# Fifteen products for eighteen in the gate and value stage of a SwiGLU block behind a gated linear attention

## The chip, the cores and the metric

The kernel runs on one core of a Trainium2 chip. The metric is the device time of one execution in microseconds. Three runs of the kernel before gave a median of 641.87 us (641.79 to 645.67). The profile was taken of one more execution.

## The reference

An attention with a decaying state (4 batches, 8 heads, 768 positions, 48 channels a head) is followed by a SwiGLU block (384 to 1536 to 384 channels). The inputs q, k, v and f_logit are float32; the three weights come as float64 and are turned into float32 on the chip.

```
f = 1.0 / (1.0 + np.exp(-f_logit))
for t in range(S):
    state = f[:, :, t, :, None] * state + np.einsum('bhd,bhe->bhde', k[:, :, t], v[:, :, t])
    y[:, :, t] = np.einsum('bhd,bhde->bhe', q[:, :, t], state)
x = y.transpose(0, 2, 1, 3).reshape(B * S, H * D)
g = x @ w_gate
silu = g * (1.0 / (1.0 + np.exp(-g)))
out = (silu * (x @ w_val)) @ w_out
```

## The kernel before

**Tiling.** The 768 positions are cut into six blocks of 128. Block c holds these 128 positions of all four batches, 512 tokens in all (TB), laid channels first in `xT[c]` as three slices of 128 channels (KT = 3). A unit is one batch of one block; there are 24, four to a block. This text counts blocks from 1 to 6, so block 1 is c = 0 in the code; units are counted from 0, and unit 8 is the first of block 3.

**Staging.** The attention of block 1 comes first. From then on the MLP of a block runs mixed with the attention of the block after it: `take_turns` (L885) deals out the pieces of the MLP and between them the 16 attention steps of the next block (`attention_steps`, L612). Block 6 has no attention beside it. The first two blocks transpose f, k and q on TensorE; from block 3 on (`SQUARES`, L315) they are loaded in a layout that VectorE transposes in 32 by 32 squares (L494, L514, L515). Their sigmoid (L493) is on ScalarE, which also does the Silu of the MLP and copies out of PSUM.

**The MLP of block 1** is plain (`mlp_plain`, L641): for each 128 of the 1536 hidden channels, three matmuls of 512 tokens for gate and three for val. **The MLP of blocks 2 to 6** is `mlp_seven` (L730). The hidden channels are cut into halves, the tokens into halves of 256 (TH), and of the three channel slices the first two form, with these halves, a 2 by 2 by 2 product that takes seven multiplications in place of eight; the third slice is added by four plain ones. `pair(j)` makes one pair of hidden tiles (128 channels of either half, so six pairs a block) by 11 products; each product is two matmuls of 256 tokens, one for gate and one for val, into the two halves of one PSUM bank (`add`, L752). VectorE adds the parts up in SBUF (`plus`, L702). The weight sums it needs are made once, after block 1, on VectorE (`weight_sums`, L711), the token sums once a block (`token_sums`, L737). A hidden tile `h[j]` has four parts of 256 tokens.

**The output product** (`down_seven`, L798) also takes seven products for eight, over sums `s1`, `s2` of hidden parts that `hidden_sums` makes behind each pair. Its four pieces `one` to `four` end a block.

**What sets the order.** [...] The order in the code is a wish: the framework that builds the program may move an instruction that is ready ahead of one that is not, by durations that it assumes. `in_order` (L621) pins the order of TensorE's instructions within a pair or an output piece. In the trace such moves can be seen: in block 6 four matmul instructions of `two` (`o<-ws,ht`, 611.65 us) run between the two halves of `one`.

**Memory.** [...] The pools of the raw inputs, the gates, tails and four v tiles live as long as the kernel; only the staging of the weights (`wst`) is given up after block 1, and the weight sums take its place. The squares layout lies over the raw inputs (`rooms`, L334). `load_after` (L606) starts the loads of a coming unit: two units ahead in the first two blocks, one ahead from block 3 on, and the loads of unit 8 during unit 7.

Of the kernel before, what the change touches and what calls it, by code (L numbers as in the profile page):

```python
# [289 lines left out]
def short_path(ctx, tc, ident, least, judge, q, k, v, f_logit, moe_w_gate, moe_w_val, moe_w_out, out):  # L290
# [29 lines left out]
    ffn = ctx.enter_context(tc.tile_pool(name="ffn", bufs=2))  # L320
    early = ctx.enter_context(ExitStack())
    wst = early.enter_context(tc.tile_pool(name="wst", bufs=2))
    aps = ctx.enter_context(tc.tile_pool(name="aps", bufs=4, space=bass.MemoryType.PSUM))
    fps = ctx.enter_context(tc.tile_pool(name="fps", bufs=4, space=bass.MemoryType.PSUM))
# [9 lines left out]
    rooms = {nm: const.tile([128, NRAW * H * W], FP32, tag=f"{nm}raw", name=f"{nm}raw") for nm in "qkf"}  # L334
    raw = {nm: [rooms[nm][:, i * H * W:(i + 1) * H * W].rearrange("t (h d) -> t h d", d=W) for i in range(NRAW)]
# [7 lines left out]
    gates = [const.tile([128, HP * N1 + 2], FP32, tag=f"gates{i}", name=f"gates{i}") for i in range(NROT)]  # L343
    tails = [const.tile([128, HP * N1 + 2], FP32, tag=f"tails{i}", name=f"tails{i}") for i in range(NROT)]
# [25 lines left out]
    vs = [const.tile([128, H, W], FP32, tag=f"v{i}", name=f"v{i}") for i in range(NV)]  # L370
# [3 lines left out]
    w_gate = const.tile([128, KT, DFF], FP32, tag="w_gate", name="w_gate")  # L374
    w_val = const.tile([128, KT, DFF], FP32, tag="w_val", name="w_val")
# [11 lines left out]
    RUN = NI * D  # L387

# [7 lines left out]
    def load(u):  # L396
# [11 lines left out]
        nc.sync.dma_start(out=vs[u % NV][:, :, 0:D], in_=v[b, :, rows, :].rearrange("h t d -> t h d"))  # L408
# [66 lines left out]

    def bank(name):
        return aps.tile([128, 512], FP32, tag="a", name=name)

    def attention(u):
        b, c = units[u]  # L480
        fr, kr, qr = (raw[nm][u % NRAW] for nm in "fkq")
        v_ = vs[u % NV]
        gate, tail = (x[u % NROT] for x in (gates, tails))
# [122 lines left out]
    def load_after(u):  # L606

        for w, ahead in ((u + 1, True), (u + 2, False)):
            if w < len(units) and (units[w][1] >= SQUARES) == ahead:
                load(w)  # L610
# [10 lines left out]
    def in_order(since, engines):  # L621

        start = len(traced)
        while traced[start - 1] is not since:
            start -= 1
        for engine in engines:
            mine = [ins for ins in traced[start:] if ins.engine == engine]
            for a, b in zip(mine, mine[1:]):
                tc.add_manual_dep(b, a.name, mybir.DependencyInfo(mybir.DependencyClass.NoSync,
                                                                  mybir.DependencyReason.DATA), reason="order")  # L630
# [67 lines left out]

    sums = {}
    down_sums = {}  # L700

    def plus(dst, a, b):  # L702
        nc.vector.tensor_tensor(dst, a, b, ALU.add)  # L703

    def minus(dst, a, b):
        nc.vector.tensor_tensor(dst, a, b, ALU.subtract)

    def temps(shape):
        return (comb.tile(shape, FP32, tag="u", name="u", bufs=2), comb.tile(shape, FP32, tag="u5", name="u5"))

    def weight_sums():  # L711
        for nm, w in (("g", w_gate), ("v", w_val)):
            s = comb.tile([128, 3, FH], FP32, tag=f"s{nm}", name=f"s{nm}")
            a11, a12, a21, a22 = w[:, 0, 0:FH], w[:, 1, 0:FH], w[:, 0, FH:DFF], w[:, 1, FH:DFF]
            plus(s[:, 0, :], a21, a22)
            minus(s[:, 1, :], s[:, 0, :], a11)
            minus(s[:, 2, :], a12, s[:, 1, :])
            minus(a21, a11, a21)
            sums[nm] = s
# [78 lines left out]
    def down_seven(c, h):  # L798
# [36 lines left out]
        def one():  # L835
# [9 lines left out]
            for j in range(NP):  # L845
                hidden_sum_4(j)
# [194 lines left out]
```

## Time and profile before

| what | us |
|---|---|
| median of 3 runs | 641.87 |
| the profiled execution | 642.91 |
| its span, first to last instruction | 641.2 |
| TensorE busy | 632.4 |
| VectorE busy | 471.0 |
| ScalarE busy | 186.6 |
| GpSimd busy | 22.4 |

The stages of the profiled execution, cut where TensorE's work changes (TensorE is busy for the whole of each stage but the first, the last, and 0.2 us of block 5):

| stage | from, to | us | VectorE busy | ScalarE busy |
|---|---|---|---|---|
| attention of block 1 | 0.0, 35.9 | 35.9 | 27.0 | 13.2 |
| block 1 | 35.9, 149.3 | 113.4 | 99.7 | 51.2 |
| block 2 | 149.3, 251.0 | 101.7 | 80.9 | 33.9 |
| block 3 | 251.0, 352.5 | 101.5 | 77.2 | 29.4 |
| block 4 | 352.5, 454.0 | 101.5 | 77.2 | 29.4 |
| block 5 | 454.0, 551.8 | 97.8 | 64.6 | 18.2 |
| block 6, gate and val | 551.8, 607.9 | 56.1 | 35.4 | 9.5 |
| block 6, output | 607.9, 641.2 | 33.3 | 8.9 | 1.8 |

In the profile PE is TensorE, PEld its weight loads, DVE VectorE, ACT ScalarE, POOL GpSimd, SP the engine whose queue issues most loads. A line number is that of kernel.py, and a helper's line stands for all its callers: L760 is the matmul in `add` of a pair, L824 that of the output product, L703 `plus`, L706 `minus`, L768 ScalarE's copy of the first product, L775 and L790 the Silus. A float32 matmul stands as two instructions, so a product of a pair (gate and val) counts four. [...]

### The profile page before, as it was taken

The page shows a single profiled execution, that of the slowest core. Times are in us where ns is not written, and L with a number is a line of the kernel's source. Part 1 is how long each engine was busy: PE and PEld are TensorE (multiplying, and loading weights), DVE is VectorE, ACT ScalarE, POOL GpSimd, SP SyncE. Part 2 cuts the span into 40 slices and gives each one's busy share as a digit, 9 for nine tenths or more (in the row PEclk, how much of TensorE's full clock was granted, in tenths as well). Part 3 has the DMA queues.
Part 4 walks back from the last instruction along what each step waited for, and adds up shares of the span by engine and source line. Part 5 has one row for each costly group of instructions (what it writes and reads, how often), then busy time and mean ns, then how long its engine had stood idle before and what let it go on. Part 6 is the DMA issues. An engine that isn't in the chain of part 4 may idle for free.

```text
span 641.2 us, 10398 instructions
## 1 busy us (share of the span) xinstructions
PE 632.4 (99%) x4014; PEld 522.3 (81%) x4014; DVE 471.0 (73%) x802; ACT 186.6 (29%) x284; POOL 22.4 (3%) x39
## 2 busy tenths in 40 slices
PE   8999999999999999999999999999999999999996
PEld 5954555667888899888999888899888889988896
DVE  6889779988987875896966787877497862366631
ACT  1566366204632212523221614130321210021100
POOL 1000000000000010010000010000000000000000
PEclk9999999999999999999999999999999999999999
DMA  9987456333230324130324321132411001100001
GB/s 193 234 212 225 127 141 206 102 81 101 67 92 6 94 67 132 50 75 26 75 52 131 91 49 50 32 80 65 123 38 49 15 24 23 54 0 1 0 1 54
DMA packets 98393, 51.89 MB, mean 81 GB/s; under 512 B 56864, under 2 KB 92192, under 8 KB 98336
## 3 DMA queue, kind: packets, MB, share of 16 engines
q1 hardware_dynamic: 95024, 46.63, 28.7%
q10 hardware_dynamic: 3312, 4.52, 2.0%
q8 instruction: 33, 0.54, 0.4%
q14 instruction: 24, 0.20, 0.1%
HBM read 42.47 MB, written 4.72 MB: 74 GB/s over the span
## 4 chain that ended last, share of the span: by engine, by line
PE 98%; DMA 1%; DVE 0%; SPq 0%; issue 0%
PE p L760 32%; PE o L824 19%; PE c L760 13%; PE o L671 5%; PE val L647 5%; PE gate L647 5%; PE sc L535 4%; PE y L565 3%; PE o L877 3%; PE y L561 2%; PE kt L542 2%; PE dS L589 2%; PE y L582 1%; DMA fraw<-in_f_logit_dram 1%; PE idle L356 1%; PE fTp L488 1%
## 5 line engine op out<-in xcount | busy, mean ns | idle before, releaser
L703 DVE TENSOR_TENSOR rest<-u,p 128x512 f32<-128x512 f32 x90 | 61.2, 685 | 43.8 <-PE p L760 43.4
L760 PE MATMUL p<-xT,w_val 128*128 128x256 f32 x240 | 71.4, 379 | 0.0
L760 PE MATMUL p<-xT,w_gate 128*128 128x256 f32 x240 | 71.4, 379 | 0.0
L703 DVE TENSOR_TENSOR u<-u,p 128x512 f32<-128x512 f32 x90 | 61.9, 687 | 10.4 <-PE p L760 8.5
L824 PE MATMUL o<-w_out,h 128*128 128x192 f32 x360 | 62.0, 329 | 0.0
L790 ACT ACTIVATE h<-rest 128x768 f32<-128x768 f32 x30 | 25.3, 844 | 123.6 <-DVE rest L703 123.6
L824 PEld LDWEIGHTS o<-w_out,h 128*128 128x128 f32 x360 | 58.2, 190 | 1.7 <-ACT u L842 1.1
L760 PE MATMUL c<-xT,w_gate 128*128 128x256 f32 x180 | 54.9, 387 | 0.0
L760 PE MATMUL c<-xT,w_val 128*128 128x256 f32 x180 | 53.5, 379 | 0.0
L760 PEld LDWEIGHTS p<-xT,w_val 128*128 128x128 f32 x240 | 45.6, 190 | 6.2
L760 PEld LDWEIGHTS p<-xT,w_gate 128*128 128x128 f32 x240 | 45.6, 190 | 6.2
L537 DVE TENSOR_TENSOR A<-sc,causal 128x512 f32<-128x512 f32 x48 | 31.5, 685 | 10.4 <-PE sc L535 10.4
L760 PEld LDWEIGHTS c<-xT,w_val 128*128 128x128 f32 x180 | 34.2, 190 | 4.6
L527 POOL TENSOR_TENSOR decayed<-state,tails 128x192 f32<-128x192 f32 x20 | 19.7, 986 | 504.3 <-DVE state L593 360.2
L760 PEld LDWEIGHTS c<-xT,w_gate 128*128 128x128 f32 x180 | 32.5, 190 | 5.2 <-issue 0.9
L760 PE MATMUL p<-xs,sv 128*128 128x256 f32 x120 | 35.7, 379 | 0.0
L760 PE MATMUL p<-xs,sg 128*128 128x256 f32 x120 | 35.7, 379 | 0.0
L791 DVE TENSOR_TENSOR h<-h,rest 128x768 f32<-128x768 f32 x30 | 28.8, 962 | 9.1 <-ACT h L790 9.1
L768 ACT COPY u<-c 128x512 f32<-128x512 f32 x30 | 17.4, 581 | 53.8 <-PE c L760 32.1
L647 PE MATMUL val<-xT,w_val 128*128 128x512 f32 x72 | 32.3, 594 | 0.0
L647 PE MATMUL gate<-xT,w_gate 128*128 128x512 f32 x72 | 32.3, 594 | 0.0
L502 DVE TENSOR_TENSOR_SCAN tails<-gates,ones 128x516 f32<-128x516 f32 x24 | 29.4, 1224 | 3.9 <-POOL decayed L527 2.1
(127 smaller groups left out, 1076.6 us busy)
## 6 DMA issues: line engine op xcount, KB each, us to landing
fraw<-in_f_logit_dram SPq DMA_DIRECT2D x64, 96.0 KB, 3.0
kraw<-in_k_dram SPq DMA_DIRECT2D x64, 96.0 KB, 2.2
qraw<-in_q_dram SPq DMA_DIRECT2D x64, 96.0 KB, 2.2
v<-in_v_dram SPq DMA_DIRECT2D x24, 192.0 KB, 3.5
w<-in_moe_w_gate_dram SPq DMA_DIRECT2D x6, 768.0 KB, 4.6
w<-in_moe_w_val_dram SPq DMA_DIRECT2D x6, 768.0 KB, 5.1
w<-in_moe_w_out_dram SPq DMA_DIRECT2D x6, 768.0 KB, 5.6
out_dram<-ob ACTq DMA_DIRECT2D x23, 192.0 KB, 2.5
```

The costliest lines, as they stand in the source:

```text
L502: nc.vector.tensor_tensor_scan(tail[:, 0:n][:, ::-1], gate[:, 0:n][:, ::-1], ones[:, ::-1], 1.0, op0=ALU.mult, op1=ALU.add)
L527: nc.gpsimd.tensor_tensor(decayed[:, :, 0:D], states[b], whole.broadcast_to((128, HP, D)), ALU.mult)
L535: nc.tensor.matmul(sc[par][:, a * C:(a + 1) * C], lhsT=kT[r, a, :], rhs=qT[r, a, :], start=True, stop=True)
L537: nc.vector.tensor_tensor(A[:, par], sc[par].rearrange("p (a t) -> p a t", t=C), causal.unsqueeze(1).broadcast_to((128, HP, C)), ALU.mult)
L565: nc.tensor.matmul(place(a, par), lhsT=v_[:, 2 * a + par, :], rhs=A[:, par, a, :], start=False, stop=a >= HP - 2, skip_group_check=True)
L647: nc.tensor.matmul(p, lhsT=w[:, i, j * 128:(j + 1) * 128], rhs=xT[c][:, i, :], start=(i == 0), stop=(i == KT - 1))
L671: nc.tensor.matmul(p, lhsT=h[n // 2][:, n % 2 * 2 + b // 2, b % 2 * C:(b % 2 + 1) * C], rhs=w_out[:, j, :], start=(n == 0), stop=(n == NF ...
L703: nc.vector.tensor_tensor(dst, a, b, ALU.add)
L760: nc.tensor.matmul(p[:, n, :], lhsT=lhsT, rhs=rhs, start=first and n == 0, stop=last, skip_group_check=True)
L790: nc.scalar.activation(h[j][:, 1:4, :], rest[:, :, 0, :], AF.Silu)
L791: nc.vector.tensor_tensor(h[j][:, 1:4, :], h[j][:, 1:4, :], rest[:, :, 1, :], ALU.mult)
L824: nc.tensor.matmul(p[:, n, :], lhsT=lhsTs[j][:, n * C:(n + 1) * C], rhs=rhs[:, j, :], start=first and j == 0 and n == 0, stop=last and j = ...
```

## The change

In blocks 2 to 6 `mlp_fifteen` takes the place of `mlp_seven`. The hidden channels are cut into thirds of 512 (`NG`), the three channel slices all take part, and the tokens stay in halves: a 3 by 3 by 2 product with fifteen multiplications in place of eighteen. `triple(j)` makes six hidden parts (128 channels of each third, both token halves), so a block has four triples, each cut into three pieces of five products.

The products of a triple run in the order of `PRODUCTS`. Six are summed up in one PSUM bank (A, two buffers), five in another (B, one buffer), two stand alone (o), and two are summed in a bank c (o and c share two buffers). Where a result needs a sum as it stands midway, ScalarE copies the bank to SBUF, and the next product of that chain is added into the bank afterwards. VectorE combines the copies. `chained` pins the order of a triple's matmuls.

The weight sums are 16 operations over both weight matrices, in place but for six new tiles; the columns of triples 0 and 2 are made by GpSimd at the end of block 1's gate and val stage, those of triples 1 and 3 by VectorE after block 1. The triples run in the order 0, 2, 1, 3. There are eleven token sums a block for four. The output product is unchanged but for where its hidden sums are made.

Raw inputs, second gates and tails, two v tiles and the old PSUM pools are given up after block 1. The squares rooms are new tiles made then (`make_rooms`, with a memset on GpSimd), the loads of unit 8 are issued then, the attention of blocks 3 to 6 has one gates tile, one tails tile and two v tiles, and it has three PSUM banks for four; the MLP has five for four.

```diff
@@ -318,10 +318,13 @@
+    sums_pool = ctx.enter_context(tc.tile_pool(name="sums", bufs=1))
+    first_pool = early.enter_context(tc.tile_pool(name="first", bufs=1))
-    aps = ctx.enter_context(tc.tile_pool(name="aps", bufs=4, space=bass.MemoryType.PSUM))
-    fps = ctx.enter_context(tc.tile_pool(name="fps", bufs=4, space=bass.MemoryType.PSUM))
+    aps = early.enter_context(tc.tile_pool(name="aps", bufs=4, space=bass.MemoryType.PSUM))
+    fps = early.enter_context(tc.tile_pool(name="fps", bufs=4, space=bass.MemoryType.PSUM))
...
+    def make_rooms(pool):
+        for nm in "fkq":
+            rooms[nm] = pool.tile([128, Q + HP * RUN], FP32, tag=f"{nm}squares", name=f"{nm}squares")
+            nc.gpsimd.memset(rooms[nm][:, HP * RUN:], 0.0)
...
@@ -605,9 +622,9 @@
-        for w, ahead in ((u + 1, True), (u + 2, False)):
-            if w < len(units) and (units[w][1] >= SQUARES) == ahead:
-                load(w)
+        w = u + (1 if units[u][1] >= SQUARES else 2)
+        if w < len(units) and (units[w][1] >= SQUARES) == (w == u + 1):
+            load(w)
...
@@ -696,27 +715,61 @@
+    def weight_sums(odd, engine):
+        w, e = weight_parts()
+        w = {n: every_second(t, odd) for n, t in w.items()}
+        e = [every_second(t, odd) for t in e]
...
+        sub(e[0], a11, a12)
+        add(e[1], a12, a33)
+        add(e[1], e[1], a13)
+        sub(e[2], e[1], a11)
+        sub(e[3], e[0], a13)
+        add(e[4], a21, a32)
+        sub(e[5], a12, a21)
+        sub(a11, a12, a23)
+        add(a13, e[3], a21)
+        add(e[3], e[3], a23)
+        add(a13, a13, a31)
+        sub(a13, a13, a33)
+        sub(a21, a22, a21)
+        add(a22, a22, a23)
+        add(a22, a22, a32)
+        sub(a31, a32, a31)
...
+    PRODUCTS = [("A", "a11", "t14"), ("B", "a23", "t8"), ("o", "a21", "b22"),
+                ("A", "a12", "t2"), ("B", "e3", "b32"), ("o", "e0", "t1"),
+                ("A", "e5", "t9"), ("B", "e2", "t5"), ("c", "a13", "b11"),
+                ("A", "e4", "t4"), ("B", "a33", "t15"), ("c", "a31", "t10"),
+                ("A", "a32", "t11"), ("B", "e1", "t3"), ("A", "a22", "b21")]
...
+        def triple(j):
+            cols = slice(j * 128, (j + 1) * 128)
...
+            def product(r):
+                name, a, b = PRODUCTS[r]
+                fresh = name == "o" or name not in p
+                if fresh:
+                    p[name] = both(name)
+                for n in range(2):
+                    nc.tensor.matmul(p[name][:, n, :], lhsT=weights_of[a][:, n, cols], rhs=tokens[b],
+                                     start=fresh and n == 0, stop=True, skip_group_check=True)
...
+            def aside(name):
+                return copy(name, "aside", bufs=3)
+
+            def finish(i, n, src):
+                dst = out_part(i, n, j)
+                nc.scalar.activation(dst, src[:, 0, :], AF.Silu)
+                nc.vector.tensor_tensor(dst, dst, src[:, 1, :], ALU.mult)
+
+            def some(n, m):
+                for r in range(n, m):
+                    product(r)
+                    if r == 0:
+                        got[11] = copy("A", "c11", bufs=2)
+                    elif r == 1:
+                        got[22] = copy("B", "c22")
+                    elif r == 2:
+                        minus(got[22], p["o"], got[22])
+                    elif r == 3:
+                        got[12] = copy("A", "c12")
+                    elif r == 4:
+                        plus(got[12], got[12], aside("B"))
+                    elif r == 5:
+                        minus(got[12], p["o"], got[12])
+                        finish(0, 1, got[12])
+                    elif r == 6:
+                        minus(got[22], got[22], aside("A"))
+                        finish(1, 1, got[22])
+                    elif r == 7:
+                        got[32] = copy("B", "c32")
+                    elif r == 8:
+                        got[31] = copy("c", "c31")
+                    elif r == 9:
+                        plus(got[32], got[32], aside("A"))
+                    elif r == 10:
+                        minus(got[31], got[31], aside("B"))
+                    elif r == 11:
+                        minus(got[32], got[32], p["c"])
+                        finish(2, 1, got[32])
+                    elif r == 12:
+                        minus(got[31], got[31], aside("A"))
+                        finish(2, 0, got[31])
+                    elif r == 13:
+                        plus(got[11], got[11], p["B"])
+                        finish(0, 0, got[11])
+                    else:
+                        finish(1, 0, p["A"])
+
+            return [lambda n=n: chained(made, lambda: some(n, n + 5)) for n in (0, 5, 10)]
...
+        order = list(range(0, NJ, 2)) + list(range(1, NJ, 2))
+        pieces = [token_sums] + [f for j in order for f in triple(j)]
+        half = 1 + 3 * (NJ // 2)
+        ready = [sorted({(i * NJ + j) % NP for i in range(KT) for j in range(n, NJ, 2)}) for n in range(2)]
+        pieces.insert(half, lambda: [hidden_sums(n) for n in ready[0]])
+        pieces.append(lambda: [hidden_sums(n) for n in ready[1]])
...
@@ -953,15 +1063,22 @@
-            pieces = hidden + last
+            pieces = hidden + [lambda: weight_sums(0, nc.gpsimd)] + last
...
         if c == 0:
             early.close()
             comb = ctx.enter_context(tc.tile_pool(name="comb", bufs=1))
-            weight_sums()
+            banks.append(ctx.enter_context(tc.tile_pool(name="bps", bufs=3, space=bass.MemoryType.PSUM)))
+            banks_a, banks_b, banks_o = (
+                ctx.enter_context(tc.tile_pool(name=f"{n}ps", bufs=k, space=bass.MemoryType.PSUM))
+                for n, k in (("A", 2), ("B", 1), ("o", 2)))
+            make_rooms(comb)
+            load(SQUARES * B)
+            down_weight_sums()
+            weight_sums(1, nc.vector)
```

## The prediction

> **What bounds the kernel now.** I read the page's busy row and the chain that ended last, first.
>
> ```profile
> span 641.2 us, 10398 instructions
> PE 632.4 (99%) x4014; PEld 522.3 (81%) x4014; DVE 471.0 (73%) x802; ACT 186.6 (29%) x284; POOL 22.4 (3%) x39
> PE 98%; DMA 1%; DVE 0%; SPq 0%; issue 0%
> ```
>
> TensorE is busy throughout and the chain is 98% its own work: the time is a count of matmuls, as long as nothing makes TensorE wait. The same chain, in order of time, gives the price in block 6, where no attention is mixed in:
>
> ```profile
> 570.79 1.73 PE p L760 x8
> 572.52 1.73 PE c L760 x8
> 574.25 5.18 PE p L760 x24
> ...
> 580.29 1.73 PE p L760 x8
> ...
> 607.92 23.59 PE o L824 x144
> ```
>
> One pair is 44 instructions from 570.79 to 580.29, 9.50 us without a gap: 0.216 us an instruction, 0.863 us a product (four of them). Next, busy time by stage (us, then PE, PEld, DVE, ACT, POOL): gate and val of block 3, its output stage, gate and val of block 6.
>
> ```profile
> 250.99:317.24 66.25, 66.25 (x418) 56.86 (x418) 53.12 (x91) 23.31 (x33) 2.38 (x2) 1.00 0.25 62
> 317.24:352.49 35.25, 35.25 (x289) 33.43 (x289) 24.07 (x45) 6.12 (x11) 2.62 (x2) 1.00 0.33 86
> 551.80:607.90 56.10, 56.10 (x261) 49.38 (x261) 35.41 (x61) 9.48 (x17) 0.00 (x0) 1.00 0.01 4
> ```
>
> VectorE is 80% busy beside the attention, ScalarE 35%: both have room to be late. The groups give the durations used below:
>
> ```profile
> L703 DVE TENSOR_TENSOR u<-u,p 128x512 f32<-128x512 f32 x90 | 61.9, 687 | 10.4 <-PE p L760 8.5
> ...
> L768 ACT COPY u<-c 128x512 f32<-128x512 f32 x30 | 17.4, 581 | 53.8 <-PE c L760 32.1
> ```
>
> Last, ScalarE's time line, where Silu and sigmoid alternate, and GpSimd's beside VectorE's:
>
> ```profile
> 288.60 0.39 ACT L775 ACTIVATE h<-c 128x256 f32<-128x256 f32 x1 [2.87 <-PE c L760]
> 289.00 1.28 ACT L493 ACT_TABLE_LOAD   x1
> 290.30 0.63 ACT L493 ACTIVATE fraw<-fraw 128x512 f32<-128x512 f32 x1
> 290.95 1.28 ACT L790 ACT_TABLE_LOAD   x1
> ```
>
> ```profile
> 131.00 0.52 POOL L527 TENSOR_TENSOR decayed<-state,tails 128x192 f32<-128x192 f32 x1 [14.02 <-DVE state L593]
> ...
> 328.60 1.31 POOL L527 TENSOR_TENSOR decayed<-state,tails 128x192 f32<-128x192 f32 x1 [20.21 <-DVE state L593]
> ```
>
> ```profile
> 328.37 1.23 DVE L522 TENSOR_TENSOR_SCAN head<-gates,start 128x516 f32<-128x516 f32 x1
> ```
>
> A sigmoid takes ScalarE for 1.91 us, with its table, and 1.28 us more before the next Silu. The same GpSimd operation takes 0.52 us alone and 1.31 us beside a scan: it ends 0.31 us after the scan does.
>
> [...]
>
> **The change part by part.**
>
> *Products.* 11 products in six pairs (66 a block) become 15 in four triples (60). Six products fewer by 0.863 us are 5.18 us a block; five blocks: **25.9 us off TensorE**, all on the path. Width and type of the matmuls stay, so the price holds.
>
> *VectorE.* A triple has nine operations of 512 (0.687 us) and six multiplications of 256 (0.415 us): 8.7 us, 34.7 a block. The six pairs had 36 of 512, six of 256 and six of 768 (0.962 us), 33.0. Eleven token sums for four at 0.42 us add 2.9 us; the hidden sums stay 24. Together +4.6 us: block 3 goes from 77.2 of 101.5 us to 81.8 of 96.3, 85%. That is hidden as long as no copy waits for it.
>
> *ScalarE.* Ten copies (0.581 us) and six Silus (0.384 us) a triple are 8.1 us, 32.5 a block, for 10.9 now. Gate and val of block 3 then hold 45 us of ScalarE in some 61 us. It fits, but these copies have a deadline now.
>
> *The new wait.* Before a chain can go on, its copy must be over. In block 6 the data of a product reach VectorE 0.20 us after its last slot (slot over at 557.68, operation at 557.88), a copy is 0.58 us, TensorE follows 0.04 us after a copy (612.34, 612.38), and a weight load leads its matmul by 0.21 us: 1.03 us. Along the chains two other products, 1.73 us, lie between a product and the next one of its bank, so a copy may queue for 0.69 us. Only at the end of a triple (products 13 and 15, both A) is there one product, 0.86 us: 0.17 us short, and 1.0 us short when the Silu of the c result, which waits for VectorE, stands ahead of that copy on ScalarE. I take 0.3 us for each of 20 triples, **+6 us**; bounds 0 (an attention matmul put in between) and 20.
>
> *Sigmoids.* Sixteen units bring 1.91 us and then 1.28 us of ScalarE between copies that can wait 0.69 us. Uncovered, a unit costs 1.2 us for the sigmoid and 0.6 for the Silu's load; with the scores and transposes (1.7 us of TensorE) or y and dS (2.1 us) just there, nothing. I take a quarter of the first, 0.3 us a unit, **+5 us**; bounds 0 and 29.
>
> *The change of pools after block 1.* On VectorE 8 weight sums (134.0 to 141.0 us) become 16 of 512: 11 us for 7. The loads of unit 8 leave block 1, and with them some 7.7 us of its early work on VectorE, so VectorE is no later. [...] The last join of w_val ends at 100.0 us[...]. Block 2 starts at 149.3 us and its third product needs the 13th sum. Behind these sums on GpSimd stand the `decayed` of unit 7, on which y waits, and the memsets of the rooms, on which unit 8's 13 loads on SP's queue wait, and behind those its sigmoid, in ScalarE's order. Block 1's output matmuls (18.3 us at the end) cover most of it. I take **+4 us**; bounds 0 and 15.
>
> *At nothing.* Two v tiles for four and one gates tile for two: their last readers are done when the next unit's turn comes, and TensorE has no wait on v now; at worst a load's landing, 3.5 us, once or twice. Three PSUM banks for the attention: scores take two and the transposes of k one, inside an 0.9 us product of cover; without it, one 0.69 us evacuation a unit, 11 us in all. The hidden sums moved into the first output piece: 12 operations of 0.425 us beside 24 matmuls of 0.33 us. The matmul start of block 2 must wait for block 1's output banks, 0 to 2 us, inside the 4 above.
>
> *Sum.* −25.9 + 6 + 5 + 4 = −10.9 us on the profiled execution's 642.9 us (span 641.2 and 1.7 around it): **632 us**. That execution lies 1.0 us above the median; I leave the difference in the range.
>
> **The rivals.** *ScalarE becomes the hub (slower).* [...] a Silu that waits for VectorE holds up the copies behind it. VectorE runs 85% full and has scans and transposes of 1.1 to 1.25 us in its queue, so its results come up to that much late, against 0.69 us of slack. For it: a copy in block 6 already stands behind a Silu (L768 at 561.94 us, its product ended at 560.9). Against it: the copies of now have no deadline, so the order was never put to the test, and eight chunks of attention matmuls a block let ScalarE catch up. At 1.0 us a triple (20 us), 1.2 us a unit (19 us) and 10 us at the change of pools it gives 643 − 25.9 + 49 = **666 us**; at three quarters of these waits 654 us. It decides from 1.3 us of waiting a triple on, where a block's 5.18 us are gone. I put it at 656.
>
> *GpSimd starves.* VectorE's sums run back to back[...], then the memset, unit 8's loads (4.4 us) and its sigmoid, with TensorE standing still at block 2's first products. With 13 us for the 4, the time is **641 us**. For it: nine of the twelve GpSimd operations of blocks 2 to 4 took 1.16 us or more. Against it: VectorE is rid of unit 8's early work.
>
> *The saving isn't real.* A product by accumulation into a bank with data could cost more than 0.863 us. The c11 bank of now does the same (L760 c) at the same step, so I give it no chance of its own.
>
> **How the numbers follow.** Forecast 632 us: 0.50; its own range is 620 to 637. GpSimd starves, 641: 0.16. ScalarE as the hub, 645 to 670: 0.34. A change within 1%, 6.4 us, is about what can't be told from none. Faster by more takes nine tenths of the forecast and a little of the second: 0.47; slower by more is most of the hub case: 0.32; the rest, 0.21, is the same. The range runs from 618, where the three waits are nearly nothing, to 660, half-way into the hub case.
>
> **What would show it.** Right: 1200 matmul instructions of the new products where 1320 stood (0.216 us each step); block 6's gate and val in 51 to 54 us; TensorE idle after ScalarE's copies, short and mostly before the fifteenth product; blocks 3 and 4 near 98 us. Hub: TensorE's waits lead by ScalarE's copies, with ScalarE's own idle time put down to VectorE and table loads, blocks 3 and 4 over 102 us. Starving: a hole in TensorE's row near 150 us that ends with GpSimd. Wrong altogether would be a kernel with TensorE 99% busy, near 617, or a wait I have not named, on PSUM banks of the attention or on its loads.

## The result, and the profile after

The changed kernel takes **671.88 us** (median of 4, 670.99 to 672.67) against 641.94 us for the kernel before on the same chip: a ratio of 1.0447 [1.0409, 1.0485]. The forecast was 632 us with a range of 618 to 660. It is slower by 30 us, on the other side from the forecast and beyond the range.

First the page of the kernel after: span, busy time of each engine, TensorE's granted clock in 40 slices, the chain that ended last by engine.

```profile
span 670.9 us, 10581 instructions
PE 628.1 (94%) x3894; PEld 503.5 (75%) x3894; DVE 507.5 (76%) x905; ACT 273.9 (41%) x504; POOL 48.3 (7%) x58
PEclk9999999599999799999999999999999989999999
PE 50%; DVE 20%; issue 5%; SPq 4%; ACT 4%; DMA 3%; POOL 0%; ACTq 0%; DVEq 0%; POOLq 0%
```

TensorE has 120 instructions fewer, as the change says. But its share of the span fell from 99 to 94%, and of the chain that ended last it holds 50% where it held 98%. VectorE has the largest part of the rest. The clock is low in one slice before block 2 (114 to 134 us) and dips twice later. TensorE's waits of the kernel after say what it stood for (us in total, how many, the longest):

```profile
PE B L844 <- DVE c L728: 14.4, 7, 3.8
PE o L690 <- DVE h L682: 13.0, 2, 7.3
PE A L844 <- ACT ob L695: 2.1, 1, 2.1
PE A L844 <- ACT aside L849: 1.8, 4, 0.6
```

L844 is the matmul of a product in a triple, L690 the output matmul of block 1, L849 ScalarE's copies, L728 and L731 VectorE's sums and differences, L695 ScalarE's copies of block 1's outputs (`ob`). The windows give the stages (from and to, us, then the busy us of PE, PEld, DVE, ACT and POOL, then clock, DMA share and GB/s): the end of block 1, gate and val of block 3, its output stage, gate and val of block 6.

```profile
114.50:169.39 54.89, 39.64 (x176) 22.98 (x172) 50.63 (x67) 10.36 (x17) 16.44 (x14) 0.88 0.20 58
277.39:347.74 70.35, 65.69 (x443) 54.05 (x441) 56.29 (x100) 40.72 (x79) 1.02 (x2) 1.00 0.23 60
347.74:380.96 33.22, 33.08 (x243) 31.49 (x241) 25.94 (x56) 5.35 (x10) 4.34 (x2) 1.00 0.37 97
584.66:636.57 51.91, 51.91 (x240) 44.85 (x239) 34.45 (x67) 30.69 (x62) 0.00 (x0) 1.00 0.02 5
```

Gate and val of block 6, with no attention beside it, took 51.9 us where it took 56.1, and TensorE was busy for all of it: there the saving came. In block 3 the same work holds TensorE for 65.7 of 70.4 us, and at the end of block 1 TensorE stands for 15 of 55 us.

| stage | before, us | after, us | with the saving alone |
|---|---|---|---|
| up to block 2's first product | 148.3 | 169.4 | 148.3 |
| blocks 2 to 5 | 403.5 | 415.3 | 382.8 |
| block 6 | 89.4 | 86.2 | 84.2 |
| span | 641.2 | 670.9 | 615.3 |

(Block 2 begins here with its first product, block 6 behind the last output matmul of block 5; half of its first product runs ahead of that.) So 55.6 us were lost against a saving of 25.9: **21.1 us before block 2**, **32.5 us in blocks 2 to 5**, 2.0 us in block 6. Of the 21.1, 2.1 lie at the start, where the first gate matmul came at 37.9 for 35.8 us. In the traces below it comes anywhere from 36.2 to 39.5 us with this start, and from 34.2 to 36.9 us with that of the kernel before, so one trace of each can't say how much of these 2.1 us is the change. The experiments take the two large ones apart.

The time line of the kernel after shows the first. GpSimd (POOL) makes its 16 weight sums from 102.4 us on; the columns are start, duration, engine, line, operation:

```profile
102.42 1.53 POOL L731 TENSOR_TENSOR extra<-w_both 128x512 f32<-128x512 f32 x1 [7.42 <-DVE w_both L459]
102.73 1.77 DVE L731 TENSOR_TENSOR extra<-w_both 128x512 f32<-128x512 f32 x1
104.42 1.62 DVE L457 TENSOR_SCALAR top<-top 128x768 int32<-128x768 int32 x1
119.21 2.01 DVE L458 SCALAR_TENSOR_TENSOR top<-w,top 128x768 int32<-128x768 int32 x1
122.68 0.67 DVE L682 TENSOR_TENSOR h<-h,val 128x512 f32<-128x512 f32 x1
130.76 5.16 PE L690 MATMUL o<-w_out,h 128*128 128x384 f32 x10 [5.71 <-DVE h L682]
134.31 0.68 DVE L728 TENSOR_TENSOR extra<-w_both 128x512 f32<-128x512 f32 x1
```

VectorE's sum of 512 takes 1.77 us beside GpSimd and 0.68 us at 134.31, when GpSimd is done. The scaling of 768 takes 1.62 us (0.56 in the kernel before), the two-input join 2.01 us (0.95). Each of these is longer by some 1.1 us, while GpSimd's 16 sums follow one another at 1.66 us each with no gap above 0.1 us, and the hidden products of block 1 (`h`, L682), which stand in the same queue, come late: TensorE waits 13.0 us for two of them. They themselves, with one input from PSUM (`val`), are not lengthened (0.67 us). Five of VectorE's own weight sums, which the code asks for only after block 1, run between 102.7 and 128 us as well, at about 1.75 us each: the framework had moved them ahead of the second of these hidden products, which came at 130.05 us. And behind the two waits the granted clock was 0.50 until 134 us; TensorE was busy for some 4.9 us of that, so I estimate 2.4 us lost to the clock.

The second is in blocks 2 to 5. Around one of the seven waits for bank B, in block 3:

```profile
323.99 1.03 PE L844 MATMUL B<-xT,extra 128*128 128x256 f32 x4
324.56 1.23 DVE L519 TENSOR_TENSOR_SCAN tails<-gates,ones 128x516 f32<-128x516 f32 x1 [0.69 <-POOL decayed L544]
327.52 1.23 DVE L539 TENSOR_TENSOR_SCAN head<-gates,start 128x516 f32<-128x516 f32 x1
329.59 0.68 DVE L728 TENSOR_TENSOR c<-c,B 128x512 f32<-128x512 f32 x1
330.32 1.13 PE L844 MATMUL B<-xs,w_both 128*128 128x256 f32 x4 [3.03 <-DVE c L728]
```

Product 14 fills bank B for the last time in a triple. What reads it last is not a copy by ScalarE but the sum `plus(got[11], got[11], p["B"])` on VectorE. It stands behind a unit's scans and other sums, and starts 4.6 us after the bank is full. The bank has one buffer, and the next triple's second product needs it.

### The profile page after: what moved, and what is told of

It is laid out like the page before. It is cut to its first block, busy times and chain, and to the rows that moved or that the text cites. A ratio compares the mean times of both kernels' runs of the same rounds, so it can differ in the third digit from the quotient of the medians.

```text
span 670.9 us, 10581 instructions
## 1 busy us (share of the span) xinstructions
PE 628.1 (94%) x3894; PEld 503.5 (75%) x3894; DVE 507.5 (76%) x905; ACT 273.9 (41%) x504; POOL 48.3 (7%) x58
## 4 chain that ended last, share of the span: by engine, by line
PE 50%; DVE 20%; issue 5%; SPq 4%; ACT 4%; DMA 3%; POOL 0%; ACTq 0%; DVEq 0%; POOLq 0%
PE o L933 13%; PE A L844 11%; PE B L844 9%; PE o L844 4%; SPq L593 3%; DVE c L731 3%; PE c L844 3%; PE o L690 2%; PE sc L552 2%; PE o L987 2%; PE y L582 1%; DVE qT L532 1%; DMA xT<-yT 1%; DVE c L728 1%; DVE A L554 1%
## 5 line engine op out<-in xcount | busy, mean ns | idle before, releaser
L844 PE MATMUL A<-xs,w_both 128*128 128x256 f32 x240 | 65.5, 395 | 3.7 <-ACT ob L695 2.1
L844 PE MATMUL B<-xs,w_both 128*128 128x256 f32 x160 | 43.9, 397 | 14.4 <-DVE c L728 14.4
L858 ACT ACTIVATE h<-c 128x256 f32<-128x256 f32 x100 | 40.5, 416 | 40.1 <-DVE c L731 38.0
L844 PEld LDWEIGHTS A<-xs,w_both 128*128 128x128 f32 x240 | 46.1, 197 | 11.8 <-ACT ob L695 2.7
L849 ACT COPY c<-A 128x512 f32<-128x512 f32 x40 | 23.3, 583 | 74.8 <-PE A L844 41.0
L849 ACT COPY aside<-A 128x512 f32<-128x512 f32 x60 | 35.1, 586 | 44.4 <-PE A L844 44.4
L728 DVE TENSOR_TENSOR c<-c,aside 128x512 f32<-128x512 f32 x40 | 28.1, 702 | 31.5 <-ACT aside L849 31.5
L731 DVE TENSOR_TENSOR c<-c,aside 128x512 f32<-128x512 f32 x60 | 41.7, 695 | 7.3 <-ACT aside L849 7.0
L690 PE MATMUL o<-w_out,h 128*128 128x384 f32 x96 | 35.0, 519 | 13.0 <-DVE h L682 13.0
L859 DVE TENSOR_TENSOR h<-h,c 128x256 f32<-128x256 f32 x100 | 41.1, 422 | 6.5 <-ACT h L858 6.5
L844 PEld LDWEIGHTS B<-xs,w_both 128*128 128x128 f32 x160 | 29.3, 193 | 20.9 <-DVE c L728 16.6
L844 PE MATMUL B<-xT,extra 128*128 128x256 f32 x160 | 42.3, 388 | 0.0
L731 DVE TENSOR_TENSOR c<-o,c 128x512 f32<-128x512 f32 x40 | 27.8, 694 | 18.8 <-PE o L844 17.4
L844 PE MATMUL c<-xT,w_both 128*128 128x256 f32 x160 | 41.2, 380 | 0.0
L844 PE MATMUL A<-xs,extra 128*128 128x256 f32 x160 | 41.2, 380 | 0.0
L933 PE MATMUL o<-ws,h 128*128 128x192 f32 x240 | 40.9, 326 | 0.0
L690 PEld LDWEIGHTS o<-w_out,h 128*128 128x128 f32 x96 | 18.7, 201 | 27.2 <-DVE h L682 14.8
L519 DVE TENSOR_TENSOR_SCAN tails<-gates,ones 128x516 f32<-128x516 f32 x24 | 30.5, 1270 | 8.9 <-POOL decayed L544 6.7
```

The costliest lines, as they stand in the source:

```text
L519: nc.vector.tensor_tensor_scan(tail[:, 0:n][:, ::-1], gate[:, 0:n][:, ::-1], ones[:, ::-1], 1.0, op0=ALU.mult, op1=ALU.add)
L690: nc.tensor.matmul(p, lhsT=h[n // 2][:, n % 2 * 2 + b // 2, b % 2 * C:(b % 2 + 1) * C], rhs=w_out[:, j, :], start=(n == 0), stop=(n == NF ...
L728: (engine or nc.vector).tensor_tensor(dst, a, b, ALU.add)
L731: (engine or nc.vector).tensor_tensor(dst, a, b, ALU.subtract)
L844: nc.tensor.matmul(p[name][:, n, :], lhsT=weights_of[a][:, n, cols], rhs=tokens[b], start=fresh and n == 0, stop=True, skip_group_check=True)
L849: nc.scalar.copy(t, p[name])
```

## The experiments

Ratios are to the kernel before, timed on the same chip between the runs, with 95% intervals.

### Bank B's last sum by way of ScalarE

```diff
-                        plus(got[11], got[11], p["B"])
+                        plus(got[11], got[11], aside("B"))
```

> The changed kernel, with the last use of bank B in a triple (product 14) copied aside by ScalarE instead of read by VectorE in its sum, so that VectorE no longer sets when B comes free. Theory (in blocks 2 to 5 VectorE's scans and transposes stand ahead of that sum, B has one buffer, and TensorE waits 14.4 us and then runs some 7 us at a lower clock): 12 to 20 us less, 652 to 660 us, and no wait of B on VectorE's sums. Rival (ScalarE is the hub): one more copy of 0.58 us a triple makes it slower, 672 to 680 us. Rival (only the start of block 2 matters): within 4 us of 671.9.

Measured: 661.73 us (659.82 to 662.17), ratio 1.0294 [1.0259, 1.0330]: 10.2 us less than the changed kernel, for one more copy a triple, and a little less than the 12 expected at least. TensorE's waits of this kernel:

```profile
PE B L844 <- ACT aside L849: 6.0, 5, 1.6
PE A L844 <- ACT c L849: 4.4, 7, 1.1
```

The waits for VectorE on bank B are gone. But of 14.4 us, 6.0 came back as waits for ScalarE's copy of the same bank, and bank A waits more than it did. Something makes ScalarE late too.

### The even weight sums on VectorE

```diff
-            pieces = hidden + [lambda: weight_sums(0, nc.gpsimd)] + last
+            pieces = hidden + [lambda: weight_sums(0, nc.vector)] + last
```

> The changed kernel, with all 32 weight sums on VectorE, in the same places of the program. Theory (between 102 and 130 us [...] each VectorE operation with two SBUF inputs takes about 1 us more, so block 1's hidden products come late and TensorE waits 13 us for them): although VectorE gets 11 us more work, the two waits on the hidden product before 131 us go, 6 to 14 us less, 658 to 666 us. Rival (it is VectorE's amount of work that makes block 2 late): 11 us more of it makes it slower, 676 to 684 us.

Measured: 663.57 us (663.21 to 665.18), ratio 1.0339 [1.0305, 1.0373]: 8.3 us less. VectorE does 16 sums more, and yet TensorE waits for it less. The wait of block 1's output matmuls is now this one, on a join of `w_out`, for 13.0 us on `h`:

```profile
PE o L690 <- DVE w_out L459: 3.4, 1, 3.4
```

### Both

> Both edits: bank B freed by ScalarE, and all weight sums on VectorE. If the two causes are apart, their gains add up: 640 to 652 us. If one hides the other: no better than the better of the two alone.

Measured: 650.48 us (648.08 to 652.15), ratio 1.0136 [1.0102, 1.0169]: 21.4 us less than the changed kernel, for 10.2 and 8.3 apart. The two losses stand beside each other; neither covers the other.

### The kernel before with idle sums on GpSimd

```diff
+            def beside():
+                for n in range(16):
+                    i, k = n % 3, n // 3 % 3
+                    cols = slice(i * 512, (i + 1) * 512)
+                    nc.gpsimd.tensor_tensor(spare, w_gate[:, k, cols], w_val[:, k, cols], ALU.add)
-            pieces = hidden + last
+            pieces = hidden + [beside] + last
```

> The kernel before, with 16 additions of 512 on GpSimd at the end of block 1's gate and val stage, whose results nobody uses. Theory[...]: VectorE's joins and scans there are stretched and TensorE waits in block 1: 648 to 656 us. Rival (GpSimd's sums cost nothing beside VectorE, the loss is in what waits for them): 642 to 644 us.

Measured: 652.02 us (651.34 to 653.48), ratio 1.0157 [1.0123, 1.0191]. Sums that nobody waits for cost the kernel before **10.1 us**. Its time line:

```profile
99.54 24.39 POOL L961 TENSOR_TENSOR spare<-w_gate,w_val 128x512 f32<-128x512 f32 x14 [7.86 <-DVE w_val L445]
107.01 1.51 DVE L443 TENSOR_SCALAR top<-top 128x768 int32<-128x768 int32 x1
109.98 2.02 DVE L444 SCALAR_TENSOR_TENSOR top<-w,top 128x768 int32<-128x768 int32 x1
118.08 1.65 PE L672 MATMUL o<-w_out,h 128*128 128x384 f32 x2 [5.68 <-DVE h L664]
```

The same stretched operations of VectorE (1.51 for 0.56 us, 2.02 for 0.95), and a wait on `h` of the same kind, 6.2 us in two places for 13.0, with half clock behind it until about 123 us. GpSimd takes 1.74 us a sum. That sums on GpSimd beside VectorE cost this, with nothing else of the changed kernel, is thereby shown; what the two engines meet at is not, only which operations are stretched.

### The product banks laid down ahead of the attention's

As "both", and in the order of pools A, B and o come first, then the attention's three banks.

> The kernel with both edits, and the PSUM banks of A, B, o and c taken from the pool before the attention's three. In that kernel TensorE waits 2.1 us at block 2's first product for the copies of block 1's outputs out of the bank that A gets. Theory: A gets a bank that was free long before, 2 us less, 647 to 649.5 us. Rival (the wait moves to the attention's scores, or to the token sums): 650 to 653 us.

Measured: 646.55 us (643.28 to 647.89), ratio 1.0075 [1.0054, 1.0097]: 3.9 us less than "both". Bank A no longer lies on a bank of block 1's output: the wait `A` on `ob` (2.1 us) is gone, and block 2 starts at 153.95 for 156.92 us.

### All 16 weight sums after block 1

As the run before, but no sums among block 1's pieces; after block 1 first the even sums, then the odd ones, then those of the output product, all on VectorE.

> The kernel with both edits and the banks taken first (646.6 us), and all weight sums asked for after block 1's pieces, the even columns first and the sums for the output product last, so that the joins of w_out and the attention come before them on VectorE. There TensorE waits 3.5 us in block 1 for a join that stands behind the sums. Theory (the order on VectorE in block 1): that wait goes, 642 to 645 us. Rival (the sums themselves are too much for VectorE before block 2): block 2 starts as late or later, 646 to 651 us.

Measured: **642.93 us** (641.32 to 643.96), ratio 1.0009 [0.9993, 1.0025]. Block 2 starts at 151.56 us, 3.3 us later than in the kernel before: the change of pools is nearly mended. Level with the kernel before, though, is not the saving.

### More buffers for bank B

Two buffers for B and one for o and c: in the changed kernel with the sums on VectorE and the banks first (B still read by VectorE), and in the kernel of 642.93 us; in the latter also with two for B, two for o and c, and two banks, not three, for the attention.

> The changed kernel with all sums on VectorE (663.6 us), A, B, o and c taken first, and two buffers for B and one for o and c together; VectorE reads the last B itself again. Theory (TensorE waits on VectorE because B has one buffer): the 14 us of waits of B on VectorE's sums go and some of it comes back at o and c, 648 to 657 us. Rival (VectorE is late whatever bank it reads, and with one bank for o and c TensorE waits there as often): 660 to 670 us.

> The same as the run before it in this list, with two buffers for B and one for o and c together. B is still copied aside by ScalarE at its last use. Theory (what is left in blocks 2 to 5 is the wait of B for that copy, 6.6 us): 637 to 642 us. Rival (o and c with one bank wait for VectorE instead): 643 to 650 us.

> The same with two buffers for B, two for o and c, and two PSUM banks left for the attention of blocks 3 to 6. Theory (the MLP's banks are what is short, three for four cost the attention about 1 us in blocks 2 to 6): 634 to 642 us. Rival (with two banks the scores and the transposes of k get in each other's way, a VectorE evacuation of 0.69 us and more for each unit): 645 to 660 us.

Measured: 653.41 us, ratio 1.0171 [1.0127, 1.0214]; 647.70 us, 1.0085 [1.0058, 1.0113]; 647.13 us, 1.0084 [1.0058, 1.0111]. The last two are slower than with one buffer, by 4.8 and 4.2 us. The first has no run with one buffer and nothing else changed beside it; 663.57 less the 3.9 us of the banks gives an estimate of 659.7, so where VectorE still reads B the second buffer seems worth some 6 us. The long wait of B went, and waits came back where the bank was taken from. The first wait of each of the three:

```profile
PE o L844 <- DVE c L731: 7.6, 4, 2.6
```

```profile
PE o L844 <- DVE c L731: 8.0, 5, 2.2
```

```profile
PE kt L559 <- DVE A L554: 8.2, 7, 2.1
```

Once ScalarE reads B, a bank more for it does not pay for the bank it is taken from: readers come late, and another bank shows it.

### Three attention banks in the kernel before

`aps` with three buffers for four, `fps` with five.

> The kernel before with three PSUM banks for the attention and five for the MLP, in place of four and four. The prediction costed that at nothing: 641 to 643 us. Rival (the attention's scores, cut into pieces by the lack of a bank, are part of the loss): 645 to 652 us.

Measured: 644.66 us (644.26 to 646.53), ratio 1.0043 [1.0032, 1.0054]: 2.8 us more than the kernel before on that chip, between the two expectations. In its trace 1.2 us of it arise before the first gate matmul (36.9 for 35.8 us), where the changed kernel still has four banks and where the traces scatter by as much.

### The sigmoids of blocks 3 to 6 left out

```diff
-            nc.scalar.activation(squares("f"), squares("f"), AF.Sigmoid)
+            nc.scalar.activation(squares("f"), squares("f"), AF.Copy, scale=0.44)
```

> The changed kernel with the sigmoid of the gates of blocks 3 to 6 left out: ScalarE scales by 0.44 instead, which needs no table. So 16 loads of the sigmoid's table and up to 16 of the Silu's fall away, some 40 us of ScalarE. The prediction's term: 5 us less, 665 to 668 us. The rival of the prediction (ScalarE is the hub): 15 us and more, under 657 us. VectorE as the cause: nothing to 3 us, 669 to 672 us.

With another gate the kernel also ran a slower general path, which it keeps for gates that this path does not cover and which comes behind it, so the whole time (1783.65 us, ratio 2.7762) tells nothing. In its trace this path's last output matmul starts at 660.1 us, in the changed kernel's at 662.9: 2.8 us. But in this trace block 2 began late, at 170.9 for 169.4 us, and all but the first of these sigmoids come after that. From there to the last output matmul it is 489.2 for 493.5 us: **4.3 us**, from one trace of each. What went are 18 table loads of 1.28 us (all 26 in the changed kernel's trace are at lines of Silu and sigmoid, none at a copy; it has nine for the sigmoid and nine for the Silu behind it, since the others fall where no Silu ran in between), 23 us of ScalarE and not the 40 expected. Bank B's waits stayed at 14.7 us. The sigmoids are not what holds ScalarE.

### What holds ScalarE: Silus later

In the kernel of 642.93 us the steps of TensorE in blocks 2 to 5, from the start of each matmul group to the next, are together 22.6 us longer than their instructions at the undisturbed price (0.216 us for an instruction of a product, 0.163 for one of the output, the attention's from the kernel before); in the kernel before 2.6 us, in the changed kernel 33.9. In steps over by more than 0.25 us, 13.4 us end with a copy of ScalarE. Its waits suggest the reason. ScalarE in the changed kernel, and then in that of 642.93 us:

```profile
ACT h L858 <- DVE c L731: 38.0, 33, 3.2
```

```profile
ACT h L858 <- DVE c L731: 30.5, 23, 2.8
```

For 38 us ScalarE stood still at a Silu whose argument VectorE had not made yet, with copies behind it in its queue. So the Silus that need VectorE were laid down one or two products later, behind the next copies; in a third run the changed kernel got the two-product delay and nothing else.

```diff
             def finish(i, n, src):
+                late.append((count[0] + LATE, lambda: finish_now(i, n, src)))
...
-                        finish(1, 0, p["A"])
+                        finish_now(1, 0, p["A"])
+                    run_late(count[0])
```

> The best version so far (bank B read by ScalarE, its banks first, all weight sums on VectorE after block 1; 642.93 us) with the five Silus of a triple that need VectorE's result laid down one product later, so that on ScalarE they stand behind the next copy and no longer ahead of it. In its blocks 2 to 5 the steps of TensorE that are longer than their price make 18.2 us, of which 13.4 end with a copy of ScalarE. Theory A (the copies are late because they stand behind a Silu that waits for VectorE): the waits on ScalarE's copies fall by half or more, 636 us (633 to 639). Theory B (ScalarE's copies are late because of their number, or the time comes back as waits on VectorE): 641 to 645.

> As the run before, but the Silus two products later, behind the next two copies. Theory A: as good or better, 634 us (630 to 638), with nearly no wait on ScalarE's copies left. Theory B: 641 to 647, since the hidden parts come later as well.

> The changed kernel with nothing but the Silus two products later. In it bank B's next product waits for VectorE (14.4 us) and for ScalarE's copies only 1.8 us. If VectorE's own lateness holds bank B, the order of ScalarE hardly matters: 669 us (666 to 673). If the forecast's rival was right for the changed kernel itself, that Silus ahead of copies are what costs, 655 to 662.

Measured: 641.68 us, ratio 0.9990 [0.9974, 1.0005]; 642.80 us, 1.0004 [0.9984, 1.0024]; 669.12 us, 1.0436 [1.0385, 1.0487]. By the time alone this would speak against ScalarE's order. But the time line of ScalarE in the second shows that the order had not changed where it matters:

```profile
300.37 0.59 ACT L856 COPY aside<-A 128x512 f32<-128x512 f32 x1 [1.14 <-PE A L851]
303.71 0.42 ACT L867 ACTIVATE h<-c 128x256 f32<-128x256 f32 x1 [2.76 <-DVE c L731]
304.04 0.57 ACT L856 COPY aside<-B 128x512 f32<-128x512 f32 x1
```

The copy of bank B was possible from about 301 us, when its product was out. It ran at 304.04, behind a Silu that waited 2.76 us. In the code this Silu now stands behind the copy; the framework that builds the program had moved it ahead. The idea was not tested, and the third run, without a pin too, does not speak against it either.

### The order on ScalarE pinned

The copies and Silus of the triples are held on ScalarE in the order of the code, as TensorE's matmuls already are; the delay is two or four products.

```diff
-        mine = [ins for ins in traced[n:] if ins.engine == mybir.EngineType.PE]
-        keep_order(made[-1:] + mine)
-        made.extend(mine)
+        for engine, done in ((mybir.EngineType.PE, made), (mybir.EngineType.Activation, made_act)):
+            mine = [ins for ins in traced[n:] if ins.engine == engine]
+            keep_order(done[-1:] + mine)
+            done.extend(mine)
```

> The run with the Silus two products later left the longest waits on ScalarE's copies (6.5 us in four places) as they were, since there the framework had moved one such Silu ahead of the last copy of bank B again: at 303.71 us a Silu that had waited 2.76 us for VectorE, and behind it the copy, with TensorE waiting for it. Here the copies and Silus of the triples are also pinned in the order of the code on ScalarE, so that no Silu that needs VectorE stands ahead of that copy. Theory A (ScalarE's order is what costs): the 6.5 us of bank B go, 635 us (632 to 638). Theory B (load of ScalarE, or the time comes back elsewhere): 641 to 645.

> As the run before, but the Silus four products later. Theory A: a copy then waits for nothing but its product and what ScalarE does for the attention; 632 to 636 us, and TensorE's waits on ScalarE's copies under 3 us. Theory B: 641 to 648, with the waits on VectorE and on the hidden parts grown.

Measured: with two products 638.40 us (637.20 to 640.30), ratio 0.9928 [0.9902, 0.9953], against 642.80 us for the same delay without the pin: 4.4 us for ScalarE's order alone. With four products it is **631.32 us** (631.10 to 632.74), ratio 0.9830 [0.9797, 0.9863], faster than both kernels. With two products a bank A wait of 5.3 us was left; with four, the page and TensorE's waits, among them those on ScalarE's `aside` copies, read:

```profile
span 629.7 us, 10606 instructions
PE 613.5 (97%) x3894; PEld 497.4 (79%) x3894; DVE 495.7 (79%) x921; ACT 286.0 (45%) x524; POOL 25.3 (4%) x42
PEclk9999999999999999999999999999999999999999
...
PE 76%; DVE 8%; issue 4%; DMA 4%; ACT 3%; SPq 3%; DVEq 0%; ACTq 0%
```

```profile
PE o L1001 <- DVE ob L728: 3.0, 5, 1.2
...
PE A L854 <- ACT aside L859: 0.3, 1, 0.3
```

ScalarE does the same work (286 us busy, 283 before the delay); its waits at Silus for VectorE fell from 30.5 to 8.2 us, and TensorE's on its copies nearly to nothing. Not the load of ScalarE but the order of its queue, with that of the multiplications which VectorE does behind the delayed Silus, cost 11.6 us here.

```profile
ACT h L870 <- DVE c L731: 8.2, 10, 1.5
```

### The same order in the changed kernel

The delay of four products with the order pinned, alone, and together with bank B's last sum by way of ScalarE. The change of pools stays as it was.

> The changed kernel with nothing but the Silus that need VectorE four products later and the copies and Silus of the triples pinned on ScalarE in the order of the code; bank B's last sum is still read by VectorE. Theory A (in the changed kernel bank B's wait for VectorE hides ScalarE's order, so the order alone gives back only what ends with ScalarE there): 666 us (661 to 670), the 14 us of waits of bank B on VectorE still there. Theory C (it was ScalarE's order from the start, and VectorE read bank B late because it waited for what ScalarE held up): the waits of bank B on VectorE fall below 5 us and the time is 650 us (646 to 656).

> As the run before, and bank B's last sum copied by ScalarE. Both causes in the gate and value stage are then gone, and what is left of the loss is the change of pools after block 1 (21 us by the traces): 671.9 less some 31 us of the 34.5 in blocks 2 to 6, 641 us (638 to 648). If one of the two causes covers the other and more is behind them, it stays above 652.

Measured: 660.84 us (654.93 to 662.57), ratio 1.0247 [1.0185, 1.0310]; 647.69 us (647.37 to 649.30), 1.0083 [1.0057, 1.0110]. TensorE's longest waits of the first:

```profile
PE o L690 <- DVE h L682: 13.0, 2, 7.3
PE B L854 <- DVE c L728: 7.0, 4, 2.1
```

The order alone gives back 11.0 us, and bank B's waits for VectorE halve, though its reader is the same: VectorE was late in part because of what ScalarE held up, between the two theories. In the second the 13.0 us stay and the wait of bank B on VectorE is gone. With both edits gate and val have lost their waits: 24.2 us back. The rest up to 631.32, 16.4 us, is the change of pools.

## Why the prediction was wrong

**What held.** TensorE was the bound, the price of a product held (block 6: 60 products by 0.863 us are 51.8, measured 51.9), and the saving of 25.9 us was real. VectorE's load was right: 82.2 us in block 3 for the 81.8 foreseen.

**The step that failed first: "The change of pools after block 1"**, +4 us with a bound of 15; the traces give 21.1, or 19.0 without the kernel's start, and the edits that mend it 16.4. Its working took VectorE to be "no later" and GpSimd to be the one that is held up; how long a sum of 512 takes GpSimd, no trace of the kernel before showed. In the trace after, GpSimd's stream runs back to back and takes turns with VectorE, one operation each (GpSimd starts at 102.42, 103.91, 105.59 and 107.12 us, VectorE at 102.73, 104.42, 105.96 and 107.64): VectorE's sums, scalings and joins are all lengthened by about 1.1 us, at a time when the last hidden products of block 1 stand behind them on VectorE. The kernel before with 16 idle sums shows 10.1 us from this alone. The steps that mend the rest are the sums' and the banks' places: the order of VectorE's queue (3.6 us, all sums after block 1) and bank A on a bank of block 1's output (3.9 us), for which the forecast had "0 to 2 us, inside the 4 above".

**The second: "The new wait"**, +6 us. For what it looked at the working was on the safe side: in block 6 the fifteenth product costs 0.13 us more, for 0.3, and in sum the named waits of bank A on `aside` are 1.8 us. It looked at ScalarE's copies alone, and put one Silu of c on them. It passed over two things that the diff shows. Bank B's last reader in a triple is VectorE, with scans ahead of it, and the bank has one buffer. And "That is hidden as long as no copy waits for it", said of VectorE's load, was exactly the condition that failed, in both directions: Silus wait for VectorE, copies stand behind Silus. Taken alone, bank B's reader is worth 10.2 us and ScalarE's order 11.0, together 24.2.

**Sigmoids**, +5 us: 4.3 from the traces, though with 18 table loads where the term counted 32. **At nothing**: the three attention banks cost the kernel before 2.8 us, 1.2 of them in its trace at a place where they do not apply; TensorE has no wait on v, and the hidden sums brought none either.

**The clock** was in no step. After the 3.8 us wait for bank B in block 2 TensorE ran for four products at half speed:

```profile
223.56 2.07 PE L844 MATMUL B<-xs,w_both 128*128 128x256 f32 x4 [3.80 <-DVE c L728]
225.43 1.91 PE L844 MATMUL o<-xT,w_both 128*128 128x256 f32 x4
227.13 1.91 PE L844 MATMUL A<-xs,w_both 128*128 128x256 f32 x4
228.84 1.47 PE L844 MATMUL B<-xT,extra 128*128 128x256 f32 x4
```

From start to start that is 1.7 us a product for 0.863 (a row lasts longer than the step to the next one, here 1.91 for 1.70 us), at a granted clock of 0.50 from 224.0 to 227.1 us. The wait cost 3.8 us and what came after it 3.2 more (6.7 us for four products). By the clock of the windows of blocks 2 to 5 (0.97, 1.00, 0.98, 0.98) about 7 us of them went this way. Shorter waits can do it too, as in the changed kernel with ScalarE's order pinned, in block 3:

```profile
323.72 1.13 PE L854 MATMUL B<-xs,w_both 128*128 128x256 f32 x4 [2.07 <-DVE c L728]
324.69 1.73 PE L854 MATMUL o<-xT,w_both 128*128 128x256 f32 x4
326.21 1.91 PE L854 MATMUL A<-xs,w_both 128*128 128x256 f32 x4
```

Over the traces of all kernels here, after the first 80 us, TensorE's named waits of 1.3 us and more sort like this: of 25 up to 1.74 us none was followed by a granted clock of 0.50; of 38 from 1.96 to 3.48 us, 25 were; of 16 from 3.78 us on, all. Behind all but one of these 25 the clock was low for 3.4 us, so that I estimate 1.7 us more for each. The same wait can go either way: that of bank A on `ob` at the start of block 2, 2.06 or 2.07 us in eight traces, was followed by the low clock in five. The shortest wait that the low clock followed was 1.96 us; what decides between the two outcomes, the traces do not show.

**The rivals.** "GpSimd starves" was wrong in direction: its sums were done by 129 us, and VectorE starved. "ScalarE becomes the hub" had the mechanism in words, "a Silu that waits for VectorE holds up the copies behind it", and its sign, ScalarE's idle time put down to VectorE (38.0 us). Its price of 20 us for the triples is nearly twice the 11.0 that the order gives back alone, and near the 24.2 of both edits. (The sign it took from block 6 was misread by a little: the product before the copy at 561.94 us had its last slot at 561.13, not 560.9.) What it missed is that bank B stood in front of it, so TensorE's waits name VectorE first, and that the change of pools costs about twice the 10 us it was given. Together these passed the range.

**What stays open.** The best kernel is 15 us from the full saving (642.4 less 25.9 is 616.4). 3.3 us are before block 2, 1.2 of them ahead of the first gate matmul. In blocks 2 to 6 it is 11 us; the steps of blocks 2 to 5 are over their price by 11.3 us, 2.6 of them on `ob`, the rest spread in small parts at changes between products and attention, for which no run was made. How much of the order's 7.1 us from two to four products is ScalarE's own queue, and how much VectorE's multiplications behind the same Silus, was not separated. Nor was it tried what the four-product delay without the pin, or the pin without a delay, would give.

## What to carry to other kernels

Before a chain in a single PSUM bank is read midway, write down for each bank who reads it last, what stands ahead of that read on the reader's queue, and how many buffers cover it; where an engine keeps the order of its queue, as ScalarE did here (a copy that was possible from 301 us ran at 304.04, behind a Silu that waited), a result that needs another engine belongs behind the copies that the bottleneck waits for, and the order must be seen in the trace, since the code's order alone did not hold. Work put on GpSimd to relieve VectorE is priced by what VectorE does meanwhile: here 16 free sums cost 10 us.

## What the hardware showed

Side by side, GpSimd and VectorE ran by turns, one whole operation each. GpSimd's sums of 512 took 1.66 us each in the changed kernel and 1.74 in the kernel before with idle sums; meanwhile VectorE's own went from 0.68 to 1.8 us, its scalings from 0.56 to 1.6 and its joins from 0.95 to 2.0. Those with an input from PSUM were not stretched: the hidden product took 0.67 us, two of the scores' (`A`) together 1.27 beside GpSimd at 109.58 us and 1.28 in the kernel before. And a stall of TensorE of 2 us cost nearly twice its length through the clock (an estimate: 3.4 us at 0.50 behind it are 1.7 us), or nothing more: of 38 waits of 1.96 to 3.48 us, 25 were followed by half clock.
